# Weight tiles in halves, the keys' memory as three more of them, and the end of the attention loop written in another order

## The chip, the cores and the metric

The kernel runs on one core of a Trainium2 chip. The metric is the device time of one execution in microseconds (us). The engines are PE (TensorE matmul; PEld are its weight loads), DVE (VectorE), ACT (ScalarE), POOL (GpSimd) and SP (SyncE, which here only issues DMAs). Each engine works through its own instructions in the order in which they were written; engines wait for each other through semaphores. A difference of under 0.2% (2.5 us) can hardly be told from no change with this kernel.

## What is computed

Top-32 attention, then a mixture of experts that sends each token to one expert. Cut to what matters:

```python
# q, k, v: 8 batches, 8 heads, 576 tokens, 64 columns
scores = (1 / sqrt(64)) * q @ k.T
kth = the 32nd largest score of each row
attn = softmax(where(scores >= kth, scores, -1e9))
x = (attn @ v)                       # as 4608 rows of 512
e_idx = argmax(x @ w_gate)           # one of 8 experts for each row
for e in range(8):
    m = e_idx == e
    h = maximum(x[m] @ w1[e], 0)     # w1: 8 x 512 x 1024
    out[m] = gate[m] * eom[m, e] * (h @ w2[e])   # w2: 8 x 1024 x 512
```

All arrays are float32, 2 MiB for each w1[e] and for each w2[e].

## The kernel before

**The attention loop.** There are 36 tiles of 128 rows with 4 pairs of heads each, so 144 steps (`NSTEP`). A step does the scores of a later pair (`scores`), the search for the 32nd largest (`rank`, `spot`, `pick`, `choose`), the exponentials (`weigh`), the transposes of the probabilities (`flip`) and every second step the product with v (`attend`). After the last pair of a tile `tile_rows` turns its result back into rows, finds the logits of the experts (two pieces of PE work, `gates` and `rows`, taken from the list `side`) and stores the rows in `x_rows`. After each group of tiles `group_route` sends the token numbers to the lists of their experts (`ids`).

**The expert work: slots.** A slot is 128 tokens of one expert. While the loop is running, full lists are taken as slots (`slot_picks`, `queue_slots`): 31 of them. What remains is nine more (`USUAL`), which are known only when the last tile has been routed (`slot_table`). So there are 40 slots. For each one SP loads its weights (`fetch_w1`, `fetch_w2`: a tile of 2 MiB each, two buffers for each), its token numbers (`fetch_id`), and POOL gathers its rows (`fetch_x`). PE transposes the rows (`turn`), then there are four pieces, one in each step of the loop (`heavy_piece`): two halves of the up product (`up`), two halves of the down product (`down`). Then ACT scales (`put`) and POOL scatters the rows to the output.

**The end.** The last 14 slots are called A to N here. A begins in step 146 of the loop, after the last `attend`, and B to E are also known by then; F to N are the nine of the table. A is done in plain float32 products, as all slots before it. After the loop `slots_in_turn` uses split products: ACT rounds a tile to a shorter float (the h of `w1h`), DVE takes the rest (`w1l`), and three quick products replace one slow product. B has its up product plain and its down product split; C to N are split throughout. A down product transposes the up product's result first (the turning of `hs`). `background` is called between PE pieces there and emits what is left of the small work: the last rows, the routing, the table. Before `slots_in_turn` the kernel calls `unsettled`, a test on all 144 steps' searches (eight DVE operations and one small PE product), whose flag decides at the very end whether a slow exact version must run too.

**Memory.** Keys (`kst`) and queries (`qst`) lie in pools that are given back together with all others of the loop at its end.

Of the kernel before, what the change touches and what calls it, by code (L numbers as in the profile page):

```python
# [23 lines left out]
P = 128  # L24
# [10 lines left out]
NLIST = 12  # L35


@with_exitstack
def tile_topk_attention_moe(
# [130 lines left out]
    def unsettled(cp, pp):  # L170
# [16 lines left out]
        nc.vector.tensor_reduce(total, bad[:1, 0, :2], axis=AX.X, op=ALU.add)  # L187
        nc.vector.tensor_copy(flag[:, 1:2], total)
        nc.vector.tensor_tensor(total, total, over, op=ALU.add)
        nc.vector.tensor_copy(flag[:, 0:1], total)  # L190

    def run(exact, stack):
# [8 lines left out]
        kv = inner.enter_context(tc.tile_pool(name="kv", bufs=2))  # L201
        wk = inner.enter_context(tc.tile_pool(name="wk", bufs=2))
# [53 lines left out]
        def load_k(b, pairs=slice(0, NHP), engs=(nc.sync, nc.sync), cols=slice(0, S)):  # L256
            if b not in K:
                K[b] = kv.tile([P, NHP, S], F32, name="kst")
# [6 lines left out]
        def load_q(t, pairs=slice(0, NHP), engs=(nc.sync, nc.sync)):  # L265
            if t not in Q:
                Q[t] = wk.tile([P, NHP, P], F32, name="qst", bufs=3)
# [173 lines left out]
        def attend(i):  # L441
# [5 lines left out]
            po = ps_o.tile([P, 2, P], F32, name="po")  # L447
# [22 lines left out]
        def tile_rows(t, g, lg, j):  # L470
# [26 lines left out]
            def rows(ps):  # L497
# [106 lines left out]
        def slot_picks(g):  # L604
# [49 lines left out]
            if eng is nc.vector:  # L654
                return [key, top, pick, total, slots, taken]
# [86 lines left out]
        def fetch_w1(s, g, k, rows):  # L742
            ev = nc.values_load(SLOT[g][0:1, 0, k:k + 1], engines=[SP], min_val=0, max_val=E - 1,
                                skip_runtime_bounds_check_because="clamped to the last expert")
            a = pools["mp"].tile([P, NC, FF], F32, name="w1t", bufs=2)
            nc.sync.dma_start(a, w1[bass.ds(ev, 1)].rearrange("o (c p) f -> p (o c) f", p=P))
            W.setdefault(s, [None, None])[0] = a

        def fetch_w2(s, g, k, rows):
            ev = nc.values_load(SLOT[g][0:1, 0, k:k + 1], engines=[SP], min_val=0, max_val=E - 1,  # L750
                                skip_runtime_bounds_check_because="clamped to the last expert")
            b = pools["mp"].tile([P, NF, DM], F32, name="w2t", bufs=2)
# [573 lines left out]
```

## Time and profile before

| | |
|---|---|
| median of 3 runs | 1263.99 us (1262.61 to 1264.73) |
| the profiled execution, own time | 1263.08 us |
| its span, first to last instruction | 1261.2 us |
| mean granted TensorE clock | 0.984 |
| PE busy | 1179.9 us, 94% of the span |
| DVE busy | 1175.4 us, 93% |
| ACT busy | 1017.7 us, 81% |
| POOL busy | 722.3 us, 57% |
| DMA | 227.39 MB, mean 180 GB/s |

Busy shares are averages over a loop of some 1057 us and an end of some 200 us, whose limits differ, so each is read by itself. The time of an execution is 1.9 us more than its span. Rows give times from the start of the span.

### The profile page before, as it was taken

What the parts mean: (1) busy time and instruction counts of PE and PEld (TensorE: products, weight loads), DVE (VectorE), ACT (ScalarE), POOL (GpSimd) and SP (SyncE); (2) the same over time, 40 slices, a digit from 0 to 9 for tenths busy, and PEclk for the clock granted to TensorE, in tenths of its full rate; (3) what the DMA queues carried; (4) which work ended last, traced back from release to release, by engine and by line L of the source; (5) the groups of instructions that cost most, each with busy time, mean ns of one, the idle gap of its engine ahead of it and who ended that gap; (6) DMA issues with size and microseconds to landing.
All of it is one profiled execution on the core that took longest, in us unless ns stands there. A gap on an engine that the chain in (4) does not pass through costs nothing.

```text
span 1261.2 us, 31032 instructions
## 1 busy us (share of the span) xinstructions
PE 1179.9 (94%) x9769; PEld 895.1 (71%) x9769; DVE 1175.4 (93%) x6189; ACT 1017.7 (81%) x1958; POOL 722.3 (57%) x1048
## 2 busy tenths in 40 slices
PE   6888788779999999999999999999999999899996
PEld 5665566557777777777777777777777777678885
DVE  7999999999999999999999999999999993789984
ACT  6999999897887878788888788788887884388883
POOL 5767677675557665665675576557557663232110
PEclk8999999999999999999999999999999999899999
DMA  5400210236446465656557546554444446899981
GB/s 139 78 18 23 68 56 18 56 142 223 168 167 210 170 215 188 211 198 226 175 205 225 191 169 209 179 204 168 168 168 168 168 169 227 305 377 396 392 310 64
DMA packets 109375, 227.39 MB, mean 180 GB/s; under 512 B 14854, under 2 KB 33542, under 8 KB 108176
## 3 DMA queue, kind: packets, MB, share of 16 engines
q1 hardware_dynamic: 99824, 205.67, 47.6%
q0 software_dynamic: 7552, 18.96, 4.2%
q8 instruction: 79, 1.29, 0.4%
q10 hardware_dynamic: 1824, 0.67, 0.2%
q14 instruction: 96, 0.79, 0.2%
HBM read 206.68 MB, written 20.69 MB: 180 GB/s over the span
## 4 chain that ended last, share of the span: by engine, by line
PE 63%; DVE 24%; issue 8%; ACT 2%; POOL 1%; DMA 1%; POOLq 0%; SPq 0%; DVEq 0%; ACTq 0%
PE pm L790 16%; PE pm L805 14%; PE po L460 10%; PE ps L282 9%; PE pst L428 9%; DVE cand L311 8%; DVE v L364 4%; DVE ep L401 3%; DVE cand L322 2%; DVE v L319 2%; PE pm L1118 1%; PE pst L480 1%; DVE v L374 1%; DMA w1t<-in_w_dram 1%; POOL xg L769 1%
## 5 line engine op out<-in xcount | busy, mean ns | idle before, releaser
L349 POOL TENSOR_TENSOR w<-s,marks 128x576 f32<-128x576 f32 x288 | 366.0, 1292 | 183.9 <-ACT marks L346 146.6
L311 DVE MAX8 cand<-s 128x8 f32<-128x72 f32 x2304 | 346.5, 219 | 8.4 <-ACT s L290 8.4
L346 ACT ACTIVATE marks<-s,v 128x576 int8<-128x576 f32 x288 | 221.1, 773 | 38.2 <-DVE v L319 27.0
L428 PE MATMUL pst<-ident,ep 128*128 128x128 f32 x1296 | 207.6, 284 | 43.6 <-ACT ep L417 32.5
L436 ACT ACTIVATE pT<-pst 128x512 f32<-128x512 f32 (+1 forms) x432 | 198.7, 487 | 56.8 <-PE pst L428 56.6
L428 PEld LDWEIGHTS pst<-ident,ep 128*128 128x128 f32 x1296 | 146.1, 142 | 131.2 <-issue 53.3
L401 DVE SCALAR_TENSOR_TENSOR ep<-s,kth,ep 128x576 f32<-128x576 f32 x248 | 219.4, 915 | 0.3
L790 PE MATMUL pm<-xs,w1t 128*128 128x128 f32 x1792 | 212.8, 278 | 0.0
L790 PEld LDWEIGHTS pm<-xs,w1t 128*128 128x128 f32 x1792 | 207.2, 194 | 0.2 <-issue 0.2
L364 DVE MAX8 v<-w 128x8 f32<-128x576 f32 x288 | 203.4, 748 | 2.2 <-POOL w L349 2.2
L805 PE MATMUL pm<-w2t,ht 128*128 128x512 f32 x432 | 194.4, 593 | 0.0
L460 PE MATMUL po<-pT,v 128*64 128x128 f32 (+3 forms) x3200 | 186.7, 268 | 0.0
L282 PE MATMUL ps<-kst,qst 64*128 64x288 f32 (+1 forms) x1280 | 179.3, 428 | 6.0 <-ACT s L290 6.0
L356 ACT ACTIVATE ep<-s,v 128x576 f32<-128x576 f32 x248 | 181.9, 787 | 3.0 <-POOL v L335 3.0
L460 PEld LDWEIGHTS po<-pT,v 128*64 128x64 f32 (+1 forms) x3200 | 159.4, 137 | 33.9 <-issue 32.2
L290 ACT ACTIVATE s<-ps 128x1152 f32<-128x1152 f32 (+1 forms) x145 | 161.5, 1114 | 4.2 <-PE ps L282 3.9
L816 POOL DMA_INDIRECT out_dram<-y,idt x40 | 44.9, 1122 | 186.9 <-ACT y L812 174.1
L805 PEld LDWEIGHTS pm<-w2t,ht 128*128 128x128 f32 x432 | 78.0, 191 | 77.5 <-issue 77.5
L319 DVE MAX8 v<-cand 128x8 f32<-128x24 f32 (+2 forms) x864 | 132.6, 194 | 0.0
L282 PEld LDWEIGHTS ps<-kst,qst 64*128 64x128 f32 (+1 forms) x1280 | 97.0, 176 | 45.0 <-issue 17.1
L322 DVE MATCH_REPLACE8 cand<-v,cand 128x24 f32<-128x24 f32 (+1 forms) x576 | 97.7, 178 | 0.0
L335 POOL TENSOR_SCALAR v<-v 128x2 f32<-128x2 f32 x144 | 33.0, 229 | 75.3 <-DVE v L319 73.3
(185 smaller groups left out, 1707.7 us busy)
## 6 DMA issues: line engine op xcount, KB each, us to landing
w1t<-in_w_dram SPq DMA_DIRECT2D x40, 2048.0 KB, 8.8
w2t<-in_w_dram SPq DMA_DIRECT2D x40, 2048.0 KB, 13.8
v<-in_va_dram SPq DMA_DIRECT2D x8, 1152.0 KB, 12.8
x_rows<-xu SPq DMA_DIRECT2D x36, 256.0 KB, 2.2
qst<-in_qa_dram SPq DMA_DIRECT2D x70, 128.0 KB, 9.9
kst<-in_ka_dram SPq DMA_DIRECT2D x14, 576.0 KB, 8.0
ids<-far SPq DMA_DIRECT2D x1, 678.0 KB, 10.4
xg<-x_rows,idt POOLq DMA_INDIRECT x40, 6.6
```

The costliest lines, as they stand in the source:

```text
L282: nc.tensor.matmul(ps[qs, a, n, :288], Q[t][rows, hp, qs], K[b][rows, hp, cols], start=True, stop=True)
L311: nc.vector.max(out=c[:, 8 * g:8 * g + 8], in_=SC[i, a][:, g * GW:(g + 1) * GW])
L346: nc.scalar.activation(m.bitcast(I8).rearrange("p (s b) -> p s b", b=2)[:, :, 1], s, AF.Sign, bias=vs[:, a, PIVOT - 1:PIVOT], scale=-(1.0 ...
L349: nc.gpsimd.tensor_tensor(w, s, m, op=ALU.add)
L356: nc.scalar.activation(EP[i][:, a, :], SC[i, a], AF.Exp, bias=VV[i][0][:, a, 32:33], scale=SCALE)
L364: nc.vector.max(out=mixed(i)[:, a, :8, 1], in_=SW[i][0][a])
L401: nc.vector.scalar_tensor_tensor(e, SC.pop((i, a)), kth_col(i, a), e, op0=ALU.is_ge, op1=ALU.mult, accum_out=SM[t][:, 2 * hp + a:2 * hp + ...
L428: nc.tensor.transpose(ps[:, c - c0, :], pt[:, c * P:(c + 1) * P], ident)
L436: nc.scalar.activation(x, ps[:, :n, :], AF.Copy)
L460: nc.tensor.matmul(po[a * 64:(a + 1) * 64, k, qs], lhs, rhs, start=half and not k and not m, stop=(c == 3 and k == 1 and m == len(TT[t]) - 1))
L790: nc.tensor.matmul(ph[:, f - f0, :], w[:, c, f * P:(f + 1) * P], XS[s][:, c, :], start=(c == 0), stop=(c == NC - 1))
L805: nc.tensor.matmul(PY[s], HT[s][:, f, :], w[:, f, :], start=(f == 0), stop=(f == NF - 1))
```

## The change

- **Weights in halves.** A half is 1 MiB: half the columns of w1[e] or half the rows of w2[e]. There are five buffers `wh` during the loop (40 KiB of each partition in place of 64). `fetch_halves` loads up to five halves ahead of the ones used, a half for each piece that was done.
- **The keys' memory.** `kst` and `qst` move into a pool `kq` of their own. It is closed in step 141, after the last scores, and three more halves (`wt`) are put there, with waits of single tiles (`reuse_waits="tile"`). From there eight halves are in use.
- **The test taken apart.** The eight DVE operations are written right after the loop; the small product and the flag come later (`counted`, `flagged`).
- **One more split up product.** The loop ends a step earlier, with the first up piece of A not yet evicted (`held`). Then come A's second up piece, B's up product as a split one, and A's down product in plain form between the others. The last rows, the routing and the table are emitted from `background` between those pieces, at most 12 small operations at a time instead of 60.
- **The last two tiles' rows** are stored through POOL's queue, not SP's.
- **Picks in the loop.** DVE's step `top` is written a step after POOL's step `key`, not right behind it; the first group's update of the taken slots is written after its slots were queued.

```diff
-    def unsettled(cp, pp):
+    def unsettled(cp):
...
-        bad = pp.tile([P, 2, P], F32, name="po")
-        nc.tensor.matmul(bad[:1, 0, :2], ones[:, 0:1], lo, start=True, stop=True)
         total = cp.tile([1, 1], F32, name="total")
...
+        def counted(pp):
+            bad = pp.tile([P, 4, P], F32, name="po")
+            nc.tensor.matmul(bad[:1, 0, :2], ones[:, 0:1], lo, start=True, stop=True)
+            nc.vector.tensor_reduce(total, bad[:1, 0, :2], axis=AX.X, op=ALU.add)
+            nc.vector.tensor_copy(flag[:, 1:2], total)
+
+        def flagged():
+            nc.vector.tensor_tensor(total, total, over, op=ALU.add)
+            nc.vector.tensor_copy(flag[:, 0:1], total)
+        return counted, flagged
...
-                        nc.sync.dma_start(x_rows[t * P:(t + 1) * P, :].rearrange("p (h d) -> p h d", h=H), xu)
+                        (nc.sync if t < NTT - 2 else nc.gpsimd).dma_start(x_rows[t * P:(t + 1) * P, :].rearrange("p (h d) -> p h d", h=H), xu)
...
-                    got.append(1)
+                    got.append(step[0])
...
-            return [part(0.7, key), lambda: len(got) == 1, top, part(1.0, pick), part(0.8, total, slots), part(0.8, taken)]
+            return [part(0.7, key), lambda: len(got) == 1 and step[0] >= got[0] + 1, top, part(1.0, pick), part(0.8, total, slots), part(0.8, taken)], []
...
-        def fetch_w1(s, g, k, rows):
+        def fetch_half(n):
+
+            s, m, half = n // 4, n // 2 % 2, n % 2
+            g, k, rows = order[s]
...
+            if fetched[0] % ring[0] >= HALVES:
+                x = pools["wt"].tile([P, 4, 512], F32, name="wt", bufs=RING - HALVES)
+            else:
+                x = pools["mp"].tile([P, 4, 512], F32, name="wh", bufs=HALVES)
+            fetched[0] += 1
+            rows = slice(512 * half, 512 * half + 512)
+            src = w2[bass.ds(ev, 1), rows, :] if m else w1[bass.ds(ev, 1), :, rows]
+            nc.sync.dma_start(x, src.rearrange("o (c p) f -> p (o c) f", p=P))
+            W[s, m, half] = x
...
+            while had["w"] < min(last, used[0] + ring[0]):
+                fetch_half(had["w"])
+                had["w"] += 1
...
-        for i in range(NSTEP + 4):
+        for i in range(NSTEP + 3):
...
+            if i == NSTEP - 3:
+                keys.close()
+                pools["wt"] = stack.enter_context(tc.tile_pool(name="wt", bufs=1, side="right", reuse_waits="tile"))
+                ring[0] = RING
+                fetched[0] = HALVES
...
+            fresh = len(heavy) == 4
             ev = heavy_piece()
             if ev:
-                late.append(ev)
+                (held if fresh and i == NSTEP + 2 else late).append(ev)
...
-            fill(60)
+            fill(12)
...
+            if done is not None:
+                splitted(cur[0], 0, 0)
+                splitted(cur[0], 0, 1)
+                held.pop()()
+                ahead("x", fetch_x, 2)
+                turned(1, "p")
+                ev = up(done, 4)
+                splitted(cur[0], 1, 0)
+                ev()
+                splitted(cur[0], 1, 1)
+                fetch_halves()
...
+        counted, flagged = (None, None) if exact else unsettled(st)
+        half_done = []
+        if held:
+            heavy.clear()
+            half_done.append(cur[0] - 1)
...
-        if not settled and small_end is None and not small:
-            unsettled(st, ps_o)
-            settled = True
         for _ in slots_in_turn():
             background()
+            if counted and small_end is None and not small:
+                counted(ps_o)
+                counted = None
```

**What moves on PE after the last `attend`.** Before, these rows follow it: A's up pieces (L790), the last tile's `gates` (L489) and rows (L498, L480), A's down pieces (L805) around the routing (L562), the test's product (L185), then B's up product in plain form.

```order
L790 MATMUL pm<-xs,w1t 128x128 x16
L779 MATMUL pst<-ident,xg_123 128x128 x4
L489 MATMUL pst<-xT,wg 32x128 x4
L480 MATMUL pst<-ident,xT 128x128 x2
L790 MATMUL pm<-xs,w1t 128x128 x16
L498 MATMUL pst<-ident,lt 128x128
...
L805 MATMUL pm<-w2t,ht 128x512 x4
...
L562 MATMUL pst<-oh_17003,before_b 128x40
...
L185 MATMUL po<-lo,ones 1x2
```

After the change the same place reads as below. `pm<-xs,wt` are A's up pieces; the rows of L1153 are B's split up product, 12 products (four times the three shown) before the `gates` (L499) and 12 after them; L831 are A's down pieces, L1169 the turning of B's result.

```order
L815 MATMUL pm<-xs,wt 128x128 x16
L1131 MATMUL pm<-ident,xg_126 128x128 x4
...
L1153 MATMUL pm<-w1h,xsh 128x512
L1153 MATMUL pm<-w1l,xsh 128x512
L1153 MATMUL pm<-w1h,xsl 128x512
...
L499 MATMUL po<-xT,wg 32x128 x4
...
L508 MATMUL po<-ident,lt 128x128
...
L831 MATMUL pm<-wh,ht 128x512 x4
...
L572 MATMUL po<-oh_17382,before_b 128x40
...
L1169 MATMUL pst<-ident,hs 128x128 x8
```

The test's product comes only after C's up product (another 24 rows of L1153), and B's up product stands between A's pieces.

**What moves on DVE.** After the change the chain of the last rows, the routing and the table runs between DVE's part of the splits: below from the splits of B's w2 (`w2l`) to those of C's w1 (`w1l<-wt`).

```order
L1125 TENSOR_TENSOR w2l<-wt,w2h 128x2048
L534 TENSOR_SCALAR r<-sums 128x8
...
L525 TENSOR_TENSOR tl<-po,r 128x128
...
L592 TENSOR_SCALAR den<-den 128x4
L1125 TENSOR_TENSOR xsl<-pm,xsh 128x512
L1125 TENSOR_TENSOR w1l<-wt,w1h 128x2048
...
L578 TENSOR_TENSOR base_17424<-po,base_16121 128x40
...
L1125 TENSOR_TENSOR htl<-pst,hth 128x512 x2
L693 TENSOR_TENSOR sl_done<-place,carry_73 1x8
...
L1125 TENSOR_TENSOR w1l<-wh,w1h 128x2048
L731 TENSOR_TENSOR sl_slot<-sl_way,first_row 1x34
L735 CAST slots<-sl_slot 1x2x34
```

Before, the same chain from `tl` to `slots` stood in one piece with no split in it, the test followed it directly, and the first split came after both.

**What moves on SP.** Before, the stores of the last two tiles' rows stand ahead of the weights of B and of C:

```order
L505 DMA x_rows<-xu 128x512
...
L746 DMA w1t<-in_w_dram 128x4x1024
...
L753 DMA w2t<-in_w_dram 128x8x512
L505 DMA x_rows<-xu 128x512
...
L746 DMA w1t<-in_w_dram 128x4x1024
...
L753 DMA w2t<-in_w_dram 128x8x512
```

After the change the last store that SP still issues (tile 33) is followed by halves alone; that of A's w2 is the first row of `wh`, those of B and C follow.

```order
L515 DMA x_rows<-xu 128x512
...
L765 DMA wh<-in_w_dram 128x4x512
...
L765 DMA wh<-in_w_dram 128x4x512
...
L765 DMA wt<-in_w_dram 128x4x512
...
L765 DMA wt<-in_w_dram 128x4x512
```

**What moves on PE in the loop.** The slots themselves shift by a few steps here and there, since the planner's rules for weights and lists changed. One kind of shift repeats: a slot's rows (`xg`) are turned in the same step as a down piece (L805, after the change L831), and not in the same step as an up piece. In one place of the loop PE had, before, around the pieces of one slot:

```order
L790 MATMUL pm<-xs,w1t 128x128 x16
L428 MATMUL pst<-ident,ep 128x128 x4
L779 MATMUL pst<-ident,xg_124 128x128 x4
L282 MATMUL ps<-kst,qst 128x288 x4
...
L805 MATMUL pm<-w2t,ht 128x512 x4
L428 MATMUL pst<-ident,ep 128x128 x4
L282 MATMUL ps<-kst,qst 128x288 x4
```

and after the change, at the same step:

```order
L815 MATMUL pm<-xs,wh 128x128 x16
L438 MATMUL pst<-ident,ep 128x128 x4
L292 MATMUL ps<-kst,qst 128x288 x4
...
L831 MATMUL pm<-wh,ht 128x512 x4
L438 MATMUL pst<-ident,ep 128x128 x4
L803 MATMUL pm<-ident,xg_127 128x128 x4
L292 MATMUL ps<-kst,qst 128x288 x4
```

The turn now uses the buffer `pm` that the down piece just before it filled and that ACT reads (`y`), where it used `pst`. Of the 27 plain turns before the last `attend`, 9 take `pm` and 18 `pst` in the code before, and 13 and 14 after.

## Rows read from the trace of the kernel before

**Rows 1.** Windows of the loop: PE, PEld, DVE, ACT, POOL busy, clock, DMA share, GB/s.

```profile
500.00:600.00 100.00, 99.66 (x845) 75.48 (x842) 98.03 (x570) 81.61 (x167) 62.16 (x93) 1.00 0.63 215
```

**Rows 2.** Busy time by windows, the end of the loop and the last slots.

```profile
1057.00:1064.00 7.00, 6.75 (x56) 4.15 (x54) 0.00 (x0) 2.32 (x5) 1.70 (x2) 1.00 0.01 5
1080.10:1085.60 5.50, 0.00 (x0) 0.00 (x0) 5.16 (x20) 0.69 (x1) 4.63 (x7) 0.92 1.07 392
1085.60:1092.20 6.60, 6.58 (x35) 6.55 (x36) 2.87 (x5) 1.91 (x1) 1.30 (x3) 0.55 0.95 314
1096.10:1108.50 12.40, 12.40 (x64) 10.30 (x62) 8.35 (x6) 8.91 (x8) 0.00 (x0) 1.00 0.80 269
1108.50:1122.30 13.80, 12.55 (x60) 9.95 (x59) 12.43 (x9) 11.69 (x12) 5.39 (x3) 1.00 1.03 406
1142.26:1154.52 12.26, 12.26 (x61) 10.23 (x60) 10.88 (x8) 10.68 (x11) 2.12 (x3) 1.00 1.04 398
```

**Rows 3.** Chain that ended last, in order of time: start, length, engine and line.

```profile
1064.18 3.77 PE pm L790 x32
1067.95 0.44 PE pst L779 x4
...
1069.12 3.57 PE pm L790 x32
...
1073.02 3.44 PE pm L805 x8
1076.45 0.12 PE pst L562 x5
...
1085.62 0.19 PE po L185 x2
1085.81 6.51 PE pm L790 x32
...
1092.76 3.59 PE pm L790 x32
...
1131.34 0.87 PE pst L1134 x8
1132.21 5.49 PE pm L1118 x24
```

**Rows 4.** Timeline of PE: the first product of C's up product.

```profile
1096.09 0.47 PE L1118 MATMUL pm<-w1h,xsh 128*128 128x512 f32 x1
```

**Rows 5.** Timeline of DVE: first and last of the routing with its table.

```profile
1073.63 0.29 DVE L515 TENSOR_TENSOR tl<-pst,r 128x128 f32<-128x128 f32 x1 [19.01 <-ACT xu L483]
1082.32 0.44 DVE L725 CAST slots<-sl_slot 1x68 int32<-1x68 f32 x1
```

**Rows 6.** Waits of SP's queue from 1020 us on: total, times, longest.

```profile
SPq L505 <- POOL xu L502: 36.1, 2, 23.3
```

**Rows 7.** Waits of PE from 300 to 1057 us: total us, times, longest.

```profile
PE pm L779 <- ACT y L812: 2.8, 8, 0.4
```

**Rows 8.** DMAs from issue to landing: of L769's gathers, L761's token numbers, L753's w2t.

```profile
DMA to landing us min/median/max: 5.9/6.6/8.8
...
DMA to landing us min/median/max: 5.2/5.9/7.4
...
DMA to landing us min/median/max: 8.2/13.8/24.3
```

**Rows 9.** Busy time by windows while B's w1t (first row), then its w2t is landing.

```profile
1068.00:1072.00 4.00, 4.00 (x42) 3.63 (x41) 0.00 (x0) 1.64 (x4) 0.00 (x0) 1.00 1.02 416
1072.00:1076.00 4.00, 4.00 (x18) 2.29 (x17) 2.16 (x12) 1.10 (x3) 1.21 (x3) 1.00 1.04 392
```

**Rows 10.** Groups by line from 1045 us on: DVE's part of a half's split.

```profile
L1091 DVE TENSOR_TENSOR w2l<-w2t,w2h 128x2048 fp32r<-128x2048 f32 x26 | 59.4, 2288 | 12.0 <-ACT w2h L1090 12.0
```

More of the change, by code (lines that the diff above doesn't have):

```diff
@@ L35 @@
 NLIST = 12
+HALVES = 5
+RING = 8
 @with_exitstack
@@ L654, in slot_picks @@
             if eng is nc.vector:
-                return [key, top, pick, total, slots, taken]
+                return [key, top, pick, total, slots], [taken]
             got = []
@@ L740, in run, with fetch_halves @@
         tail = [False]
-        def fetch_w1(s, g, k, rows):
+        def fetch_half(n):
+            s, m, half = n // 4, n // 2 % 2, n % 2
+            g, k, rows = order[s]
             ev = nc.values_load(SLOT[g][0:1, 0, k:k + 1], engines=[SP], min_val=0, max_val=E - 1,
                                 skip_runtime_bounds_check_because="clamped to the last expert")
[L745 to L752, printed above, removed]
-            nc.sync.dma_start(b, w2[bass.ds(ev, 1)].rearrange("o (c p) f -> p (o c) f", p=P))
-            W.setdefault(s, [None, None])[1] = b
+            if fetched[0] % ring[0] >= HALVES:
[7 more added lines that the diff above has]
+            W[s, m, half] = x
+        fetched = [0]
+        used = [0]
+        ring = [HALVES]
+        def fetch_halves(ahead_of=None):
+            last = 4 * len(order)
+            if ahead_of is not None:
+                last = min(last, ahead_of)
+            while had["w"] < min(last, used[0] + ring[0]):
+                fetch_half(had["w"])
+                had["w"] += 1
         def fetch_id(s, g, k, rows):
@@ L800, in down @@
         def down(s, f0):
-            w = W[s][1]
+            w = W.pop((s, 1, f0 // 4))
+            used[0] += 1
             if f0 == 0:
@@ L860, in fetch_ahead @@
         def fetch_ahead():
-            for what, f in (("w1", fetch_w1), ("w2", fetch_w2)):
-                ahead(what, f, 1 if heavy else 2)
+            fetch_halves()
         def ahead_of_slot():
@@ L932, in route @@
             if g < NGRP - 1 and EARLY[g]:
-                small.extend(slot_picks(g))
+                picks, after = slot_picks(g)
+                small.extend(picks)
                 small.append(lambda: not waiting("ids"))
@@ L936, in route @@
                 small.append(lambda: step[0] >= known[0] and ids_known())
+                small.extend(after)
+        held = []
         LGT = {}
@@ L1072, in background @@
             if extra:
-                extra(ps_t.tile([P, 4, P], F32, name="pst"))()
+                extra(ps_o.tile([P, 4, P], F32, name="po"))()
                 side_use()
-            fill(60)
+            fill(12)
             run_slow(1e9, ("ids", "x", "out"))
@@ L1109, in splitted @@
             def splitted(s, m, half):
-                if s < min(len(order), had["w2" if m else "w1"]) and (s, m, half) not in HL:
-                    w = W[s][m][:, 4 * half:4 * half + 4] if m else W[s][m][:, :, 512 * half:512 * half + 512]
+                if (s, m, half) in W:
+                    w = W.pop((s, m, half))
+                    used[0] += 1
                     HL[s, m, half] = parts([P, 4, 512], (("w1h", "w1l"), ("w2h", "w2l"))[m])
@@ L1137, in down_half @@
             def down_half(s, half):
+                if not isinstance(HT[s], list):
+                    down(s, 4 * half)
+                    return
                 if half == 0:
@@ L1149, in up_plain, with first_slot @@
                 nc.vector.scalar_tensor_tensor(lo, ph, 0.0, hi.bitcast(F32), op0=ALU.max, op1=ALU.subtract)
[L1151 removed]
+            def first_slot(done):
+                if had["turn"] == done:
+                    ahead("x", fetch_x, 2)
+                    ahead("turn", lambda s, *_: turn(s, pools["p"], "pm")(), 1)
+                ahead("x", fetch_x, 3)
+                cur[0] += 1
+                for half in range(2):
+                    splitted(done + 1, 0, half)
+                    up_plain(done, 4 * half)
+                    if not half:
+                        turned(1)
+                    yield
+                fetch_halves()
+                splitted(done, 1, 0)
+                splitted(done, 1, 1)
+            done = half_done.pop() if half_done else None
+            if done is None and cur[0] == len(order):
                 return
[L1153 removed]
             ahead("id", fetch_id, 3)
[L1155 to L1170 removed]
+            fetch_halves()
+            if done is not None:
+                splitted(cur[0], 0, 0)
+                splitted(cur[0], 0, 1)
+                held.pop()()
+                ahead("x", fetch_x, 2)
+                turned(1, "p")
[3 more added lines that the diff above has]
+                splitted(cur[0], 1, 1)
+                fetch_halves()
+            else:
+                done = cur[0]
+                yield from first_slot(done)
             late = True
@@ L1244, in run @@
             pass
-        if not settled:
-            unsettled(st, ps_o)
+        if flagged:
+            if counted:
+                counted(ps_o)
+            flagged()
         def more():
```

67 lines of the change are left out of this document (21 added, 46 removed).

## The prediction

> **What bounds the kernel now.** I read the busy shares by windows first, one stage at a time, because the loop and the end have different limits. In the loop PE is busy for 99.66 of 100 us and DVE for 98.03 [rows 1]: PE sets the pace, and there the change can only win what makes PE's own work shorter. In the last slots the window of one slot, 12.26 us, is filled by PE alone (12.26 of 12.26); DVE has 10.88 and ACT 10.68, and the DMA engines are busy throughout at 398 GB/s [rows 2]. So a settled slot is bound by PE, with DVE 1.38 us behind it and the transfers just keeping up.
>
> Between the two stages lies time that PE loses. The chain that ended last shows it in order [rows 3]: A's pieces stand one behind the other from 1064.18 on, the routing's small products come at 1076.45, and the next row of PE is the test's product at 1085.62. The window between shows PE with nothing to do for 5.50 us, while DVE is busy for 5.16 of them with the end of the table and the test [rows 2]. DVE's part runs from `tl` at 1073.63 to `slots`, which ends at 1082.76 [rows 5], and the test follows it. In the next window PE's granted clock is 0.55, about the lower of its two levels (1.2 against 2.4 GHz), after that pause; B's first up piece takes 6.51 us there, its second one, with the clock back, 3.59 [rows 3]. So the pause costs 5.5 us, and 2.9 us more behind it.
>
> A second loss is in the weights. SP waits 36.1 us in two waits, the longer one 23.3 us, for the rows of the last tiles (`xu`) before it may store them, and the weights queue behind those stores [rows 6]. From 1057 to 1064 the DMA engines move 5 GB/s [rows 2]. What was not fetched then is missed later: the period from C's up product to D's takes 12.40 us and the next one 13.80, of which PE works 12.55, where a settled one takes 12.26 [rows 2].
>
> **The change part by part.** The sum is made against the profiled execution: 1261.2 us of span, 1263.08 us of its own time. That is 0.9 us under the median of the runs shown.
>
> *The end written in another order.* I follow PE from the end of `attend` (1064.18), in the order that the changed code has. A's up piece 3.77 and B's turn 0.44; A's second up piece 3.57; B's split up product, 24 products for 5.49 as in a later slot, with the last tile's small pieces in and behind it (0.73 from 1068.39 to 1069.12, and 0.33 from 1072.69 to 1073.02); C's turn 0.44; A's down piece 3.44 with the routing's 0.12 behind it; the turning of B's result 0.87; A's other down piece 3.44 [rows 3]. That makes 22.6 us, so C's up product would begin at 1086.8. Before, it begins at 1096.09 [rows 4]. **−9.3 us**, if nothing waits. In it are the pause (5.5), the slow piece (2.9), and 0.9 from B's split product net of its extra turning. The test's product stands behind C's up product: **+0.2** [rows 3].
>
> Does nothing wait? The eight operations of the test now stand where DVE is idle: it does nothing from 1057 to 1064 [rows 2]. If that cover were not there, they would cost DVE about 2.9 us, from the end of `slots` to the test's product [rows 3, 5]. The routing and table, 9.1 us of DVE from `tl` to the end of `slots` [rows 5], now stand among the splits. Before `slots` come four large splits at 2.29 us each [rows 10] and a few smaller ones. With `tl` at about 1075.5, behind the logits' pieces in B's up product, 9.1 us of its own and some 11 us of splits, `slots` would end near 1096. Its token numbers land 5.2 to 7.4 us after issue and the gather 5.9 to 8.8 us after its own [rows 8], so F's rows are there between 1107 and 1112. PE wants them for F's turn behind E's up product, at 1086.8 + 2 × 12.26 + 5.5 = 1116.8. That is a margin of 5 us at least, but the chain's place on DVE is my estimate; if it were all pushed behind, F would wait some 3 us. Bounds 0 and +3; I take **+0.7**, near the end with the margin.
>
> *The weights in halves, and SP freed of two stores.* With the stores on POOL, and three halves more, SP can fetch from step 141 on without the 36 us of waiting. So I count the two long periods as settled ones: 12.40 − 12.26 and 13.80 − 12.26, **−1.7**. Bounds: −1.7 and 0.
>
> Does a transfer of 1 MiB hold the rate? The pieces of a half are 2 KB long. The trace has both forms: while w1, with pieces of 4 KB, lands, the window shows 416 GB/s, and while w2, with pieces of 2 KB as all halves now have, 392 [rows 9]. A slot moves 398 GB/s × 12.26 us = 4.88 MB [rows 2], and at 392 GB/s that takes 12.4 us, 0.2 above PE's need: at worst 2 us over nine slots. I count nothing, since the pieces are in the order of PE's use and buffers are freed one by one.
>
> The Trainium skill, "DMA: Bandwidth & Descriptors", section "Bandwidth", measures 341 GB/s for a transfer of 1 MB issued from GpSimd, against 425 for 16 MB. By that page alone a slot would take an estimated 14.3 us, and nine of them 18 us more. The rows above, with several transfers under way at once, show more than its figure.
>
> *The loop.* Five halves stand where eight halves' room stood. A half is fetched when a piece is done and used five pieces later, so it has some four steps. A step is about 1057/144 = 7.3 us, hence 29 us; the longest landing of a whole w2 took 24.3 us, the median 13.8 [rows 8]. No wait expected; it would show at once on PE, as PE has no slack. The turns are the one thing that I do charge. Four more of them use the buffer that ACT has still to read: PE waited so 8 times, 2.8 us in all, 0.35 each [rows 7]. Four times 0.35 is **+1.4**; bounds 0 and +2.8. The later `top` and the later update of the taken slots move DVE's work out of waits, not out of PE's way: nothing.
>
> **Sum.** −9.3 + 0.2 + 0.7 − 1.7 + 1.4 = −8.7. From 1263.08 that is 1254.4; from the median, 1255.3. I say **1255.0 us**. With each term at its better end (−10.8 in all) it would be 1252.3 to 1253.2, at its worse end (−9.3 + 0.2 + 3 + 2.8 + 2 = −1.3) 1261.8 to 1262.7.
>
> **The rivals.** *The routing becomes the wait.* 9.1 us of small DVE work is put into two periods that have 1.38 us to spare each [rows 2, 5]; the pause would move into DVE's column, and PE wait for splits. For it: DVE was the busier one in the long period (12.43 of 13.80). Against it: DVE is idle for 7 us just before, and can do B's splits ahead. Up to 9.1 − 2.8 = 6.3 us given back, at half of that or more 1258 to 1261.
>
> *The change doesn't do what it says.* Some small piece is still emitted last and PE pauses as before, with the low clock behind it. Then only the weights' 1.7 us can be won and the loop's 1.4 lost: 1263 to 1264. Against it: in the changed order B's twelve and twelve split products and A's two down pieces stand between the routing's steps.
>
> *It ends slower.* The rate of the transfers went from 416 to 392 GB/s when their pieces were halved [rows 9]; if halving the whole transfer costs as much twice more, it is 344. A slot takes 4.88/0.344 = 14.2 us, 1.9 more than PE needs, nine slots (F to N) 17: 1272. It decides against the change when the gain and the 2.5 us that can be told are used up, 11.2 us or 1.24 a slot: a period of 13.5 us, 361 GB/s. For it: the DMA share is 1.04, with no room. Against it: 406 GB/s in the long period [rows 2]. The figure of the Trainium skill's page named above, 341 GB/s, lies on this side of it. The same sign has a loop in which five halves don't suffice: some 30 waits of 0.4 us, one a slot, would do.
>
> **How the numbers follow.** My forecast, 1251.5 to 1258: 0.62. The routing as the wait, 1258 to 1261.4: 0.16. A better one, under 1251.5, in which PE also gains in the loop: 0.06. No effect, 1261.5 to 1266.5: 0.08. Slower, around 1272: 0.08. What this kernel's measurement can tell from no change is 0.2%, 2.5 us. The first three are all faster by more: 0.84. The range from 1251.0 to 1261.5 holds the first two and a little of the third: 8 in 10.
>
> **What would show it.** Right: no idle window of PE between 1064 and 1090, the granted clock 1.00 there, C's up product near 1087 plus what the loop shifts; periods of 12.3 us from then on, 392 GB/s or more in them; the last `attend` ended within 3 us of 1064.18. Wrong: PE waiting for DVE's splits or F's gather (the routing); long landings of the halves with PE or ACT waiting for `wh` and `wt` (the rate); in the loop, PE's waits on halves, or `attend` ending later.

## The result, and the profile after

| | before | after |
|---|---|---|
| median of 6 runs | 1263.48 us (1261.45 to 1264.73) | 1252.95 us (1252.12 to 1253.97) |
| ratio | | 0.9918, 95% interval 0.9906 to 0.9931 |
| span of the profiled execution | 1261.2 us | 1251.1 us |
| mean granted TensorE clock | 0.984 | 0.986 |

The change makes the kernel 10.5 us faster. The forecast was 1255.0 us, the range 1251.0 to 1261.5.

Busy time by windows of the changed kernel; the columns are those of [rows 1]. The first two rows are stretches of [rows 2], the others run from one slot's turn to the next.

```profile
1057.00:1064.00 7.00, 6.75 (x41) 3.90 (x41) 1.19 (x5) 2.47 (x5) 0.49 (x1) 1.00 0.52 154
1080.10:1085.60 5.50, 5.50 (x25) 2.98 (x25) 3.26 (x14) 3.27 (x6) 1.88 (x4) 1.00 1.04 393
1093.62:1106.77 13.15, 12.47 (x62) 10.18 (x61) 12.94 (x27) 11.36 (x11) 8.63 (x8) 1.00 1.04 351
1106.77:1119.06 12.29, 12.29 (x61) 10.26 (x62) 11.51 (x9) 10.21 (x10) 4.36 (x5) 1.00 0.99 342
1131.32:1143.58 12.26, 12.26 (x62) 10.23 (x61) 10.88 (x8) 10.67 (x10) 2.11 (x3) 1.00 1.04 373
1143.58:1155.84 12.26, 12.26 (x62) 10.23 (x61) 10.88 (x8) 10.67 (x10) 2.13 (x3) 1.00 1.05 390
```

The pause is gone: from 1080.10 to 1085.60 us, where PE had nothing to do, it is busy for 5.50 of 5.50 us, at a granted clock of 1.00. Between 1057 and 1064 us the DMA engines move 154 GB/s where they moved 5. A settled slot is PE's, as before, 12.26 us.

Where the gain is made is seen at the turns of the slots' rows, which mark the slots' borders. The timeline of PE, first before (D to G), then after (A's first up piece, C's first product, then D to G):

```profile
1101.66 0.60 PE L1097 MATMUL pm<-ident,xg 128*128 128x128 f32 x4
1115.03 0.60 PE L1097 MATMUL pm<-ident,xg 128*128 128x128 f32 x4
1127.99 0.60 PE L1097 MATMUL pm<-ident,xg 128*128 128x128 f32 x4
1140.25 0.60 PE L1097 MATMUL pm<-ident,xg 128*128 128x128 f32 x4
```

```profile
1065.35 3.84 PE L815 MATMUL pm<-xs,wt 128*128 128x128 f32 x32
1087.54 0.80 PE L1153 MATMUL pm<-w1h,xsh 128*128 128x512 f32 x1
1093.62 0.66 PE L1131 MATMUL pm<-ident,xg 128*128 128x128 f32 x4
1106.77 0.63 PE L1131 MATMUL pm<-ident,xg 128*128 128x128 f32 x4 [0.68 <-DMA xg<-x_rows,idt]
1119.06 0.60 PE L1131 MATMUL pm<-ident,xg 128*128 128x128 f32 x4
1131.32 0.60 PE L1131 MATMUL pm<-ident,xg 128*128 128x128 f32 x4
```

A begins 1.2 us later than before [rows 3], C 8.6 us earlier [rows 4], G 8.9 us earlier, and so does everything behind G. The last scatter of POOL confirms it, before and after:

```profile
1253.54 0.98 POOL L816 DMA_INDIRECT out_dram<-y,idt  x1 [6.67 <-ACT y L812]
```

```profile
1244.58 0.98 POOL L842 DMA_INDIRECT out_dram<-y,idt  x1 [6.65 <-ACT y L838]
```

That is 9.0 us of the 10.1 by which the spans differ. The rest lies behind the last scatter: 7.7 us to the span's end before, 6.5 after. That part need not be the change's: over the profiled executions of all the kernels below it is 7.1 us in the mean of those made from the kernel before, 7.3 in the mean of those made from the changed one.

In the loop PE waits for ACT to read `pm` (compare [rows 7]), 4 times more often, 1.4 us more:

```profile
PE pm L803 <- ACT y L838: 4.2, 12, 0.4
```

### The profile page after: what moved, and what is told of

It is laid out like the page before. It is cut to its first block, busy times and chain, and to the rows that moved or that the text cites. A ratio compares the mean times of both kernels' runs of the same rounds, so it can differ in the third digit from the quotient of the medians.

```text
span 1251.1 us, 31395 instructions
## 1 busy us (share of the span) xinstructions
PE 1177.5 (94%) x9737; PEld 891.0 (71%) x9737; DVE 1181.8 (94%) x6192; ACT 1023.9 (82%) x1962; POOL 721.8 (58%) x1050
## 5 line engine op out<-in xcount | busy, mean ns | idle before, releaser
L359 POOL TENSOR_TENSOR w<-s,marks 128x576 f32<-128x576 f32 x288 | 367.2, 1296 | 195.5 <-ACT marks L356 161.5
L438 PE MATMUL pst<-ident,ep 128*128 128x128 f32 x1296 | 207.1, 284 | 40.7 <-ACT ep L427 30.8
L438 PEld LDWEIGHTS pst<-ident,ep 128*128 128x128 f32 x1296 | 145.9, 142 | 128.0 <-issue 52.7
L411 DVE SCALAR_TENSOR_TENSOR ep<-s,kth,ep 128x576 f32<-128x576 f32 x248 | 224.2, 934 | 0.3
L815 PE MATMUL pm<-xs,wh 128*128 128x128 f32 x1664 | 195.0, 275 | 0.0
L831 PE MATMUL pm<-wh,ht 128*128 128x512 f32 x424 | 190.7, 592 | 0.0
L815 PEld LDWEIGHTS pm<-xs,wh 128*128 128x128 f32 x1664 | 189.9, 192 | 0.0
L292 PE MATMUL ps<-kst,qst 64*128 64x288 f32 (+1 forms) x1280 | 180.0, 429 | 6.0 <-ACT s L300 6.0
L831 PEld LDWEIGHTS pm<-wh,ht 128*128 128x128 f32 x424 | 76.4, 190 | 76.0 <-issue 76.0
L292 PEld LDWEIGHTS ps<-kst,qst 64*128 64x128 f32 (+1 forms) x1280 | 97.4, 176 | 45.2 <-issue 17.5
L421 POOL TENSOR_TENSOR w<-s,marks 128x576 f32<-128x576 f32 x40 | 51.9, 1297 | 40.0 <-ACT marks L418 39.7
```

The lines of the kernel that those rows point to most:

```text
L292: nc.tensor.matmul(ps[qs, a, n, :288], Q[t][rows, hp, qs], K[b][rows, hp, cols], start=True, stop=True)
L359: nc.gpsimd.tensor_tensor(w, s, m, op=ALU.add)
L411: nc.vector.scalar_tensor_tensor(e, SC.pop((i, a)), kth_col(i, a), e, op0=ALU.is_ge, op1=ALU.mult, accum_out=SM[t][:, 2 * hp + a:2 * hp + ...
L438: nc.tensor.transpose(ps[:, c - c0, :], pt[:, c * P:(c + 1) * P], ident)
L815: nc.tensor.matmul(ph[:, f - f0, :], w[:, c, (f - f0) * P:(f - f0 + 1) * P], XS[s][:, c, :], start=(c == 0), stop=(c == NC - 1))
L831: nc.tensor.matmul(PY[s], HT[s][:, f, :], w[:, f - f0, :], start=(f == 0), stop=(f == NF - 1))
```

## The experiments

Each time is a median; each ratio is against the kernel before (1263.0 to 1263.2 us in these groups of runs). "The changed kernel" is 0.9918.

**The test alone.** In the kernel before, only the test is taken apart: its eight operations stand right after the loop, the product at the old place.

```diff
+        counted = None if exact else unsettled(st)
         while heavy:
             background()
...
-            unsettled(st, ps_o)
+            counted(ps_o)
             settled = True
```

> The kernel before, with the test's eight DVE operations written right after the loop and only its small product left at the old place. Theory (PE's pause ends when DVE has done the test): the pause of 5.50 us shrinks by the test's 2.9 us to about 2.6; the time falls by 2.9 us if the clock still drops behind a shorter pause (about 1260.6), by 5.8 us if it holds (about 1257.7). Rival (the routing and the table or a transfer set the pause, the test only lies beside them): under 0.5 us of difference. Second rival (what PE gains here it loses waiting for weights in the two long periods, 12.40 and 13.80 us): the pause shrinks, those periods grow by as much, and the time falls by under 1 us.

1258.43 us, ratio 0.9961 (0.9947 to 0.9974). The theory's second time, 1257.7, lies inside that interval, but by luck: PE's pause did not shrink to 2.6 us, it went altogether, and part of that gain was lost again further on. The timeline of PE, from the test's product on:

```profile
1079.20 0.19 PE L188 MATMUL po<-lo,ones 128*1 128x2 f32 x2
1079.32 3.84 PE L793 MATMUL pm<-xs,w1t 128*128 128x128 f32 x32
...
1088.26 0.49 PE L1121 MATMUL pm<-w1h,xsh 128*128 128x512 f32 x1 [1.09 <-ACT xsh L1093]
1089.61 0.50 PE L1121 MATMUL pm<-w1l,xsh 128*128 128x512 f32 x1 [0.86 <-DVE w1l L1094]
1090.81 0.79 PE L1121 MATMUL pm<-w1h,xsl 128*128 128x512 f32 x1 [0.69 <-DVE xsl L1094]
1091.40 0.63 PE L1121 MATMUL pm<-w1h,xsh 128*128 128x512 f32 x1
```

The product waits for nothing, and B's up pieces follow it at full speed (3.84 for 6.51 us in [rows 3]). Nothing on PE there needs the routing or the table; it was the product alone that stood in PE's order before B's work and needed a DVE that was busy with both. PE gets to C 8 to 9 us sooner and now has to wait there: the products wait for C's splits, with pauses of about 1 us, and the clock is low again (0.68 granted from 1089.0 to 1092.5, products of 0.63 us for 0.39). The chain that ended last says what is behind it:

```profile
1074.08 0.33 SPq L508
...
1074.98 10.19 DMA w1t<-in_w_dram
...
1085.32 1.92 ACT w1h L1093
```

SP issues C's weights only after the last store (L508). So the second rival was right in kind and too large in size: 4.8 us are kept, and some 3.6 lost, if the pause and the low clock together were 8.4.

**The clock alone.** In the kernel before, useless transposes fill the pause:

```diff
+        warm = pp.tile([P, 2, P], F32, name="po")
+        for c in range(48):
+            nc.tensor.transpose(warm[:, c % 2, :], ident, ident)
         bad = pp.tile([P, 2, P], F32, name="po")
```

> The kernel before, with 48 transposes of no use on PE (about 0.11 us each, 5.3 us) ahead of the test's product, where PE has nothing to do for 5.50 us. Theory (the pause itself lets the clock fall): the granted clock stays 1.00 behind the pause, B's first up piece takes 3.6 us instead of 6.5, and the time falls by 2.9 us to about 1260.6, or by less if PE then waits for weights. Rival (the piece is slow because it waits for weights or shares the chip's memory with transfers): it still takes about 6.5 us, no difference.

1260.83 us, ratio 0.9978 (0.9969 to 0.9987):

```profile
1080.61 5.40 PE L186 MATMUL po<-ident 128*128 128x128 f32 x48
1086.39 0.19 PE L188 MATMUL po<-lo,ones 128*1 128x2 f32 x2 [0.37 <-DVE lo L183]
1086.51 3.84 PE L793 MATMUL pm<-xs,w1t 128*128 128x128 f32 x32
```

The same wait for DVE ends at the same point of the program, but PE was busy up to 0.37 us before, B's piece takes 3.84 us, and the granted clock from 1085.60 to 1092.20 is 1.00, where it was 0.55 [rows 2]. So 2.4 of the expected 2.9 us are the price of the clock, and PE's earlier pause is its cause.

**Stores on POOL, whole weights.** The first experiment, with one line more:

```diff
-                        nc.sync.dma_start(x_rows[...], xu)
+                        (nc.sync if t < NTT - 2 else nc.gpsimd).dma_start(x_rows[...], xu)
```

> The kernel before with the test's eight operations right after the loop, and the last two tiles' rows stored through POOL's queue; weights still whole. With the early test alone the pause of 5.5 us and the low clock's 2.9 us were gone, but the time fell by 4.8 us only: 3.6 us went to waits for C's and E's weights, which were issued behind the stores. Theory (those weights are late because SP's queue stands at the stores): with the stores off SP's queue C's weights come some 10 us earlier, the 3.6 us come back, and the time is about 1254.5 to 1256. Rival (whole weights have too few buffers; only the halves with three more buffers help): within 1 us of the early test alone, 1258.4.

1254.94 us, ratio 0.9939 (0.9925 to 0.9952): 3.5 us more, as the theory had it. C's products now follow without a wait. ACT still waits for w1 of the first slots, 7.4 us in three waits, and PE for D's instead of C's, so that D's turn to E's takes 15.2 us.

**Two transfers for each tile.** In the kernel before, each weight tile of 2 MiB is fetched by two transfers of 1 MiB; the buffers are the same.

```diff
-            nc.sync.dma_start(a, w1[bass.ds(ev, 1)]...)
+            for f in (slice(0, 512), slice(512, 1024)):
+                nc.sync.dma_start(a[:, :, f], w1[bass.ds(ev, 1), :, f]...)
```

(and w2 by halves of its rows)

> The kernel before with each of its transfers of 2 MiB issued as two of 1 MiB into the same buffer, so that all pieces are 2 KB long; nothing else. Theory (PE sets the settled slots and the rate stays above 385 GB/s): slots remain at 12.26 us, the long period D to E grows by under 1 us since it waits for w1 (416 GB/s in pieces of 4 KB before, 392 by w2's), the time is within 1.5 us of the kernel before. Rival (smaller transfers cost rate: 361 GB/s or less): settled slots of 13.3 us and more, 9 us slower or more, about 1272.

1260.12 us, ratio 0.998 (0.9971 to 0.9989). Faster, which neither expected. Two of its windows, the slot from D's turn to E's and a settled one:

```profile
1101.60:1113.86 12.26, 12.26 (x61) 10.23 (x60) 10.89 (x8) 10.44 (x10) 2.45 (x2) 1.00 0.93 340
1152.26:1164.52 12.26, 12.26 (x62) 10.23 (x61) 10.88 (x8) 10.68 (x11) 2.13 (x3) 1.00 1.05 386
```

The settled rate is 386 GB/s for 398 [rows 2], and costs nothing: PE has no gap. It is also no sign of a slower transfer. A slot needs two tiles of 2 MiB, 128 gathered and 128 scattered rows of 2 KiB, 4.72 MB, and in 12.26 us that is 385 GB/s. The kernel before moved more than a slot needs; that it was making up for late weights is likely, but was not shown. The long periods are gone: from turn to turn, D to E and E to F took 13.37 and 12.96 us, and both take 12.26 here, 1.8 us less. The rest of the difference between the two profiled executions lies behind the last scatter. What is gained is that the first half can be split as soon as it has landed: of D's w1, ACT splits the first half at 1102.77 and the second at 1105.56, where both stood at 1105.36 before. ACT's waits for w1 from 1050 us on, before and here:

```profile
ACT w1h L1090 <- DMA w1t<-in_w_dram: 9.6, 3, 5.1
```

```profile
ACT w1h L1092 <- DMA w1t<-in_w_dram: 5.1, 3, 3.0
```

**All three in the kernel before.**

> The kernel before with the test's operations right after the loop, the last two stores on POOL, and each weight transfer issued as two of 1 MiB; four whole buffers, B's up product plain, end of the loop as before. Theory (three small edits hold nearly all of the gain; the last slots then don't wait for weights): the 8.4 us of pause and low clock and the 1.7 us of the long periods are gone, 1263.2 - 10.1 = about 1253, as fast as the changed kernel within 1.5 us. Rival (the keys' memory and the new order are needed): no better than with whole transfers, 1254.9 or more.

(The three diffs above together.) 1253.06 us, ratio 0.9923 (0.991 to 0.9937). As fast as the change, without the keys' memory, the five buffers, the new order and the split product.

**The old order in the changed kernel.**

```diff
-        for i in range(NSTEP + 3):
+        for i in range(NSTEP + 4):
...
-                (held if fresh and i == NSTEP + 2 else late).append(ev)
+                late.append(ev)
```

> The changed kernel (halves, three more buffers in the keys' place, stores on POOL, test taken apart), but with the loop one step longer and B's up product plain again as in the kernel before, so that nothing stands between A's pieces. Theory (the order brings most): PE pauses about 2.6 us for the routing and the table; with the clock falling behind it 2.9 us more, and 0.8 us for the plain product net of the turning: 3.4 to 6.3 us slower than the changed kernel, about 1256.4 to 1259.3. Rival (the weights in halves and the stores on POOL bring most of the gain): within 1.5 us of the changed kernel.

1256.21 us, ratio 0.9945 (0.9932 to 0.9959), 3.3 us slower than the change. The size is the theory's lower end, its reason is not: PE's timeline shows B's plain pieces right behind A's down pieces, at full clock, and one wait later, for a split.

```profile
1079.02 3.68 PE L831 MATMUL pm<-wh,ht 128*128 128x512 f32 x8
1082.54 3.73 PE L815 MATMUL pm<-xs,wh 128*128 128x128 f32 x32
...
1104.62 0.50 PE L1153 MATMUL pm<-w1l,xsh 128*128 128x512 f32 x1 [1.24 <-DVE w1l L1125]
```

There is no pause in it for the order to remove. From A's first piece to F's turn it takes 55.5 us, 1.8 more than the change: 0.8 up to D's turn, as much as the plain product costs net of the turning, and 1.0 behind it, where that wait stands against the change's shorter one for a gather. The other 1.4 us are A's start, at 1066.72. The edit changes nothing in the steps before A, and A's start scatters that much by itself: it lies between 1064.6 and 1066.7 in the six profiles of kernels that have the changed kernel's loop and turns, and between 1063.3 and 1065.5 in the six with the loop of the kernel before.

**The test late in the changed kernel.** The eight operations go into `counted`, behind the table.

```diff
         def counted(pp):
+            nc.vector.tensor_scalar(gap, NEAR[:, :, :, 1], 1.0 + 2.0 ** -19, None, op0=ALU.mult)
...
             bad = pp.tile([P, 4, P], F32, name="po")
```

> The changed kernel with the test's eight DVE operations written where its small product is, behind the table, not right after the loop. Theory (it was the test in DVE's stream ahead of a product that PE met in order): PE waits for those operations at the small product behind C's up product, up to 2.9 us, and the splits behind them come later; 2 to 4 us slower than the changed kernel, 1255 to 1257. Rival (DVE has room there, the place of the operations is free once the product stands late): within 1 us of 1253.

1264.42 us, ratio 1.0013 (1.0004 to 1.0022): the whole gain is lost, 11.5 us, far more than the theory's 2 to 4. The waits of PE from 1050 us on, and two windows:

```profile
PE po L191 <- DVE lo L189: 8.2, 1, 8.2
```

```profile
1094.00:1100.00 6.00, 0.00 (x0) 0.00 (x0) 5.79 (x17) 0.00 (x0) 4.28 (x5) 0.71 1.21 293
1100.00:1106.00 6.00, 4.96 (x16) 4.09 (x17) 3.10 (x8) 2.40 (x2) 0.00 (x0) 0.50 0.82 284
```

PE's product waits not for the 2.9 us of test alone but for all that DVE has to do ahead of it, splits and table; then PE runs at the lower clock level (0.50). D's turn comes 7.5 us later than in the change, and E's 9.3.

**Stores back on SP in the changed kernel.**

```diff
-                        (nc.sync if t < NTT - 2 else nc.gpsimd).dma_start(x_rows[...], xu)
+                        nc.sync.dma_start(x_rows[...], xu)
```

> The changed kernel with all rows stored through SP's queue again. Theory (SP stands still for the two stores, 36 us in the kernel before, while weights could land): PE waits again in the first slots of the end, 2 to 5 us slower than the changed kernel, about 1255 to 1258. Rival (the eight halves fetched before suffice to cover the stores): within 1 us of 1253.

1252.28 us, ratio 0.9918 (0.9904 to 0.9931): no difference; the rival is right. SP's waits from 1020 us on are down from 36.1 us [rows 6] to

```profile
SPq L515 <- POOL xu L512: 11.2, 2, 7.2
```

and the time shows no cost of them; that the eight halves cover them is the likely reason. PE doesn't wait for E's gather here (see below): from D's turn to E's it is 12.31 us.

**Five buffers to the end.** The pool `wt` isn't opened and the ring stays at five.

```diff
-                pools["wt"] = stack.enter_context(tc.tile_pool(name="wt", ...))
-                ring[0] = RING
-                fetched[0] = HALVES
```

> The changed kernel without the three halves in the keys' place: five buffers to the end. Theory (a settled slot is PE's; the three more give the lead that the first slots need): the first slots of the end wait for weights, 1.7 to 6 us slower than the changed kernel in all, about 1254.7 to 1259; the settled slots remain at 12.26 us. Rival (with five buffers transfers can't overlap enough and the settled period grows): over 13 us a slot, 1262 or more. Second rival (five suffice): within 1 us of 1253.

1288.24 us, ratio 1.0202 (1.0189 to 1.0216): slower than the kernel before by 25 us, than the change by 35. Windows of the first slots of the end and of late ones:

```profile
1100.00:1113.40 13.40, 5.51 (x16) 3.60 (x15) 11.40 (x31) 4.41 (x4) 6.68 (x9) 0.75 1.00 325
1150.28:1164.26 13.98, 12.49 (x62) 10.21 (x61) 10.90 (x8) 10.56 (x11) 4.99 (x3) 1.00 0.97 340
1164.26:1177.88 13.62, 12.81 (x62) 10.13 (x61) 10.30 (x8) 9.95 (x11) 4.64 (x3) 1.00 0.94 321
```

D's turn comes 19.8 us later than in the change (1113.43 for 1093.62). From there three periods take 12.3 us each, and from 1150 on they take 13.6 to 14.0. ACT waits for weights from 1050 us on:

```profile
1125.76 0.60 PE L1128 MATMUL pm<-ident,xg 128*128 128x128 f32 x4
1138.02 0.60 PE L1128 MATMUL pm<-ident,xg 128*128 128x128 f32 x4
```

```profile
ACT w1h L1121 <- DMA wh<-in_w_dram: 39.9, 20, 5.2
```

The theory named the first slots, with far too small a price, and it was wrong that settled slots stay at 12.26 us: the rival's growing period is there, though not in every slot.

**Quarters.** Each half is fetched by two transfers of 512 KiB.

```diff
-            nc.sync.dma_start(x, src...)
+            for c in (slice(0, 2), slice(2, 4)):
+                nc.sync.dma_start(x[:, c, :], src[:, c, :])
```

> The changed kernel with each half issued as two transfers of 512 KiB into the same buffer; pieces of 2 KB as before. Theory (it is the length of a piece and not that of a transfer that costs rate, and PE has the settled slots): 12.26 us a slot, within 1 us of the changed kernel. Rival (the length of a transfer costs rate): a lower rate in the settled slots, periods above 12.4 us, 1.5 us slower or more.

1254.46 us, ratio 0.9942 (0.9928 to 0.9955). By the median it is 1.5 us slower, more than the theory's 1 us, but the two intervals (0.9906 to 0.9931 for the change) still overlap. The slots do not show it: a settled one is

```profile
1143.00:1155.26 12.26, 12.26 (x62) 10.23 (x61) 10.88 (x7) 10.67 (x11) 2.13 (x3) 1.00 1.05 387
```

and the last scatter starts at 1244.43, for 1244.58. At the rate that a slot needs, the length of a transfer costs nothing here.

**The turns.** In the changed kernel all plain turns of the loop use `pst`.

```diff
-                pool, name = (ps_t, "pst") if heavy else (ps_m, "pm")
+                pool, name = ps_t, "pst"
```

> The changed kernel, with every plain turn in the loop in the buffer pst, none in pm. Theory (each turn in pm behind a down piece makes PE wait 0.35 us for ACT, and PE sets the loop's pace): the 12 waits of 4.2 us in all go, the last attend ends about 4 us earlier, the time falls by 3 to 4 us to about 1249 to 1250. Rival (the loop goes at DVE's pace as well, 98 percent busy, or the turns now wait for a pst buffer): within 1 us of the changed kernel.

1248.71 us, ratio 0.9882 (0.9866 to 0.9898), 4.2 us faster than the change. The 12 waits for `y` are gone, and A's up begins at

```profile
1058.57 3.84 PE L815 MATMUL pm<-xs,wt 128*128 128x128 f32 x32
...
1101.11 0.63 PE L1131 MATMUL pm<-ident,xg 128*128 128x128 f32 x4 [1.79 <-DMA xg<-x_rows,idt]
```

6.8 us earlier; 1.1 of it goes into a longer wait for E's gather. Each wait costs more than the 0.35 us that its row shows. The same turn in both traces, in the change and then here, between the transposes ahead of it (L438) and the scores behind it (L292):

```profile
735.56 0.60 PE L438 MATMUL pst<-ident,ep 128*128 128x128 f32 x4
736.50 0.66 PE L803 MATMUL pm<-ident,xg 128*128 128x128 f32 x4 [0.34 <-ACT y L838]
737.09 1.24 PE L292 MATMUL ps<-kst,qst 64*128 64x288 f32 x8
```

```profile
732.04 0.60 PE L438 MATMUL pst<-ident,ep 128*128 128x128 f32 x4
732.48 0.60 PE L803 MATMUL pst<-ident,xg 128*128 128x128 f32 x4
733.01 1.24 PE L292 MATMUL ps<-kst,qst 64*128 64x288 f32 x8
```

From the first row's start to the last one's it is 1.53 us with the wait and 0.97 without, so the wait costs 0.56 us. In a row of matmuls without a wait, each group starts before the modelled end of the one ahead of it (732.48 for 732.64 here), and that overlap is lost as well. Twelve times 0.56 is 6.7 us, close to the 6.8 seen.

**The turns, and stores on SP.**

> The changed kernel with all plain turns in pst and all rows stored through SP's queue. Theory (the turns' waits are worth 4 us and the place of the stores nothing, since eight halves cover them): within 1 us of the version with the turns alone, 1248.7. Rival (POOL's stores delay the gather of E, for which PE waits 1.8 us in that version): 1.8 us faster, about 1247.

(Both diffs above.) 1248.61 us, ratio 0.9892 (0.9877 to 0.9907): no difference to the turns alone. E's gather is waited for 0.7 us, not 1.8, but A begins 0.6 us later, and the time shows no gain. These two are the fastest versions.

## Why the prediction was right, and where its reasons were not

**The sum.** It gave −8.7 us against the profiled execution; the last scatter starts 9.0 us earlier. Term by term:

- *−9.3 for the start of C.* From A's first piece to C's, 31.9 us became 22.2, −9.7. Right in size, and the reason was half wrong. The prediction put the gain down to "the end written in another order". The runs put 8.6 us of it (the pause and the clock behind it) down to the place of the test's eight operations: in the changed kernel with the old order, where the test is early, A to C takes 23.3 us. Moved alone, those operations remove the pause; put back alone, they bring a longer one. What the prediction had wrong is the price of that place, "they would cost DVE about 2.9 us" if their cover were gone: DVE's cost is that, but PE's product waits for everything that DVE has ahead of the test, 8.2 us in that run, and the low clock comes on top. The new order, with the split product, has the other 1.1 us; behind C it spares the wait for a split as well.
- *+0.2 for the test's product.* D's turn comes 6.08 us after C's start for 5.57 before, +0.5; the product itself is 0.2 of it. The other 0.3 is C's first product, 0.80 us for 0.47.
- *+0.7 for a late gather.* PE waits 0.68 us for a gather, but E's, not F's. POOL's timeline and its waits from 1080 us on show why:

```profile
1090.90 1.06 POOL L603 DMA_INDIRECT ids<-entry,posi  x1 [8.29 <-DVE posi L599]
...
1097.45 2.07 POOL L793 DMA_INDIRECT xg<-x_rows,idt  x1 [0.30 <-issue]
```

  E's tokens were known, but its gather is queued on POOL behind the scatter of token numbers, and that waits 8.3 us for DVE's `posi`, now written among the splits. So the rival of the routing becoming the wait was there in small, through a third engine's queue. It stands on the margin: with all stores on SP the same gather is issued behind the same scatter, and PE doesn't wait for it. F's rows, which the term was for, came in time; `slots` ended at 1098.9 for the estimated 1096.
- *−1.7 for the long periods.* The prediction read the second one 0.2 us too short. It runs from D's first up product, at 1108.48, to E's, 14.06 us and not 13.80:

```profile
1122.54 0.39 PE L1118 MATMUL pm<-w1h,xsh 128*128 128x512 f32 x1
```

  So 1.9 us were to be won. D to E went from 13.37 us (turn to turn) to 13.15 with the gather's 0.68 in it, E to F from 12.96 to 12.29: −1.6 without the gather. Right in size; the reason, "SP freed of two stores", is not needed in the changed kernel, where the stores' place makes no difference. It is what helps when weights are whole.
- *+1.4 for the turns.* 12 waits for 8, 1.4 us more by their rows, and A begins 1.2 us later; but the price of a wait was too small. At 0.56 us each, four more cost 2.2 us. A's start scatters by 2 us from profile to profile, so that 1.2 lies near 1.4 is partly luck. The price is real for all twelve, and taking them away makes a faster kernel. The bound of +2.8 that the text gave for it was no measure of what there was to win.
- *Five halves in the loop, counted at nothing.* No wait for them on PE. But the prediction gave the three more halves no part beyond the long periods, and that was far off: without them the end loses 35 us, and the change would have been a loss of 25.

**The rivals.** "It ends slower" has fallen: the seven slots from F's turn on move 355 to 390 GB/s (373 and 390 in the two shown above) in periods of 12.26 us. The sum that the rival and the term for the rate rest on was wrong, though: a slot moves 4.72 MB and not 4.88, since 398 GB/s was more than a slot needs. So the rate would have decided at 350 GB/s and not 361, and 392 suffices (12.0 us a slot). The prediction's sign "392 GB/s or more" did not come, for the same reason: a slot asks for 385. The Trainium skill, "DMA: Bandwidth & Descriptors", section "Bandwidth", has 341 GB/s for a transfer of 1 MB issued from GpSimd and asks for 1 MiB or more to a DMA. The runs here, with several transfers queued from SP, show more at both sizes: 386 GB/s with 1 MiB and 387 with 512 KiB, and these are what PE's pace asks for, not the most that could be had. That the change does nothing has fallen.

**What stays open.** The medians differ by 10.5 us, the last scatter by 9.0. The stretch from the last scatter to the end of the span is between 6.05 us (two transfers for each tile) and 8.17 us (quarters) in the profiled executions of all the kernels here, and it doesn't go with the edits. It is one execution of each, and it was not followed up. The same holds for A's start, which differs by up to 2.2 us between profiles of kernels with the same loop. Shares of under 2 us in the account above rest on one profile each.

## What to carry to other kernels

A small product whose operands come from a busy engine stops everything behind it in PE's order, for as long as that engine's queue is, not for as long as its own operands take; the operands belong where that engine is idle. That was enough here, with the product at its old place, and moving the product behind other work was not, as long as its operands came late. Price a moved step by the queue that it stands in. And before reordering the end of a kernel, take each piece alone: here three small edits of the old kernel, moving the test, the stores and the borders of transfers, made the whole gain, and the largest further gain that was found is a line about which buffer a turn uses.

## What the hardware showed that was not expected

- Splitting a transfer of 2 MiB in two cost no time (386 GB/s, where a slot needs 385) and shortened two periods by 1.8 us in all, since the first half can be split before the second has landed. The kernel became 3 us faster by the median.
- With five buffers of 1 MiB the slots from 1150 us on moved 321 and 340 GB/s and ACT waited 39.9 us for weights, where seven settled slots with eight buffers moved 355 to 390 GB/s.
- The low clock behind a pause of 5.5 us cost 2.4 us here. Three pauses of 0.7 to 1.1 us shortly after each other, ahead of C's split products in the kernel with the early test, were followed by products of 0.63 instead of 0.39 us, at a granted clock of 0.68.
- A wait of 0.34 us in PE's rows cost 0.56 us, since the overlap with the matmuls ahead is lost with it.
